# A sketched attention feeding four attention experts on one core: the written-out order of jobs redone at both ends, v spread by ScalarE, more idle matmuls at the start, and the last group finished expert by expert

## The chip, the cores and the metric

The kernel runs on one core of one Trainium2 chip. The metric is the time of one execution on the device in microseconds (us). PE is the matrix engine, DVE the vector engine, ACT the scalar engine, POOL is GpSimd, and SP issues DMAs. SBUF is the on-chip memory that all of them read; PSUM is where PE writes.

## The reference, cut to what matters

```
# block 1, for each batch b (4) and head h (4), S = 1088 rows, D = 32, r = 8
phi(x) = outer(S1 x, S2 x)              # 64 features per row
kv = phi(k)^T v ;  z = sum of phi(k) over the rows
attn = (phi(q) kv) / (phi(q) . z + 1e-6)
x = attn of the 4 heads side by side    # (4, 1088, 128)
# block 2, 4 experts, each row keeps its best 2 of logits = x @ w_gate
a_e = softmax(causal(x wq[e] (x wk[e])^T / 8))
out = sum over the two kept experts of share * (a_e x wv[e] wo[e])
```

The inputs are 32-bit floats; S1 and S2 arrive as 64-bit patterns that the kernel decodes itself.

## The kernel before, in words

**Jobs and their order.** The kernel is a list of 1270 jobs. `job(...)` (line 78) records a job's name, the engine or the engines that may do it, a planned cost, what it reads, what it makes and which buffers it holds. `Plan.run` (line 84) walks the text `ORDER` (line 21): each word is a job's number, with the letter a or b for the first or second of two engines ("-" as engine means that the job is left out). The order of the words is the order in which each engine's instructions stand, and an engine runs its instructions strictly in that order. Waits between engines are put in by the tile framework. The cost and landing figures given to `job` are only what the order was planned with: `run` doesn't use them. All DMAs are issued by SP, except three early ones by ACT.

**Front, batch 0.** `decode` (line 293) turns the bits of S1 and S2 into floats on DVE; `spread1` to `spread3` copy them to the other partitions. `dummy0` to `dummy39` (line 244) are idle matmuls, two 128x512 matmuls each on a tile of zeros; most are left out. k, q and v are loaded (lines 457 to 472); `turn k`, `turn q` transpose on DVE (line 494 and 488), `sketch q0` and `sketch k0` multiply with S on PE (line 518), `back` transposes out of PSUM on DVE (line 522), `features` forms the outer product on DVE or POOL (line 527), one job per head. `sums 0.m` adds up kv and z on PE (line 558): it needs `spread v0` and `spread v1` (line 447), which copy the loaded v into rows of 33 with a one at the end. `turn qf`/`keep qf` (lines 592, 594) turn the features of q, `numer` (line 615), `divide`, `turn x` and `keep x` give x. `turn w`, `keep w`, `products` and `keep M` (lines 378 to 409) fold wq with wk and wv with wo into Mq and Mo.

**Choice of experts.** `logits` (line 807) on PE, then `choose a`, `choose b`, `maximum` and `turn choice` on DVE (lines 827 to 888) and `shares` on POOL. Masks for group 0 of batch 0 are widened on PE by `onehot` (POOL, line 369) and `widen` (line 906); the other masks go through a DRAM tensor `md` and come back by DMA.

**Batches 1 to 3** are prepared beside the scores of the batch before: `sketch`, `features` and `sums` of k, `expand`, `repeat sums`, `fifth` and `keep rep`, `sketch q`, `weigh q`, `invert q`, `scale q`, `features q`, `turn f`, and `numer` (line 757), the PE job that gives x of the next batch.

**Scores and values.** The 17 strips of 64 rows stand in groups 0 (strips 0 to 5), 1 (6 to 11) and 2 (12 to 16). `query`, `base` and `pick` (lines 953 to 985) form the queries of the two chosen experts of each row; for each strip `score` (line 998, PE), `take` (1010, DVE: mask and running minimum), `exp` (ACT), `guard`, `invert` (DVE), `weigh` (1041, POOL) and `turn A` (1046, DVE). `sum b.n.j` (line 1074) multiplies the weights of a group with x on PE. `values` (line 1056) then makes the four experts' parts out of the two PSUM tiles: `keep V` copies, `patch V` overwrites where a row's second expert sits in the other tile, `spread V` multiplies by the masks on POOL, two experts at a time. `outputs` (line 1115) multiplies with Mo: for group 0 `out 3.0.x` does 128 rows with all four experts each (line 1144), then one `keep out` and one `store out`. Batch 3 runs its groups in the order 1, 2, 0, so that `out 3.0` is the end of the kernel.

Of the kernel before, what the change touches and what calls it, by code (L numbers as in the profile page):

```python
# [14 lines left out]
ALU = mybir.AluOpType  # L15
# [6 lines left out]
56 45 47 0 1 8a 77 60 46 3 2 76 25a 19a 17a 48 79 49 51 78 57 90 89 74 87 75 88 50 13b 98 100 99 102a 103a 91 92 83 93  # L22
97a 84 81 104b 22a 101b 113 96a 117 118a 82 111 112a 115 109 110a 94a 95a 38b 80 392 86 85 106 116a 393 114a 105 108a
107a 391 394 402 395 401 405 406 119 404 408a 54 120 124 125 129 407 130 121 66 122a 52 64 58 53 65 146 131 410a 126
411a 67b 132a 400 127a 147 152 55 68 397 396 69 123 71 150 70 148 153 155 44b 398 180 72 27b 16b 684 149 151 167 168
169 170 63 156 157a 158 685 159a 59 409b 179 184a 183a 154 162 163 181 399 185 73 182 413 412 186 414a 61 403 174 687
686 695 694 416 194 62a 415 417 195 196 420b 418b 215 216 419b 217 218a 421 222 423 9b 24b 31b 26b 422 164 219 171 128
165 137 187 188 133 172 246 173 430 431 197a 198 223 424 425 189 190a 191 245 250a 12b 166a 199 688 249a 201 202 200
318 5b 432 160 203 208 175 251 7a 426 427a 433a 224 247 192 428b 248 225a 161a 209 429 434a 210 252 319 322a 323a 193
435 698 268 226 227 700 699 204a 205 206 139 220 135 176 267 269 270 228 436 438a 207 141 703a 271b 704b 437b 324 221  # L30
211a 212 260 261 262 263a 213 275 321 276 277 278 279b 177 178b 214 253 254 456 458 272 457 273 14b 142 693 320 325
255 292 291 293 274 701a 42b 264 691 280 702a 134 136 229 230 231 459 460 692 256b 234a 284 294 283 233a 462 281 257
232a 258 265 690 689 706 705 285 286 235b 342 707a 708 237 236 239 709 710 696 713a 238 711a 712a 259 282 697 461 266
295a 296 343 326 344 297 287a 327 328 288 289 298 714 715 717 463 350 290 329 330b 716 723 724 725 345 346a 10b 143
21b 472 138 331 473 477b 718 347 351 352 35b 353 354a 144 727a 332 348 719 140 29b 439 476b 464 299 300 301 302 303
304 308a 441 306a 307a 726a 333 349 467 478 335 310 474 440 334 305b 309 475 336 479 359 337 338a 358 360 339 361 362
355 468 508 509 442 720a 984 311 312 540 721a 363 340 501 364a 443 502 480 979 341 481 482 541 314 465 487 365 488 356
357 483a 315 313 366 367 538 494 977 978 495 980 316a 981 728 539 542a 368 369 370 987 496 503 504a 145 371 372 373
374 317 469 375 470 543a 544 545 471a 505 506 985 988 484 485 486 497b 444 498 722 499 510 511b 489 490a 491 512 513
376 379b 447 500 380a 515 383 516 553 377a 381 445 554 492 493 378a 382 448 584 585 586 517 518a 729 555 449 446 453  # L40
982 983 730a 514 519 731b 451 991 520 521 993 749 556b 992 994b 587 588a 569 546 996b 750 384 385 997a 507 557 558 547
751 548 386 568 989 522 589 523 524 549a 550 551 559 570 571 526a 752 753 590 242 591 525a 754 611 529 995a 530 241
528b 527a 531 612 616a 561 760 732 452 387 615a 755 455 466 733 572a 756 560 573 574 389 614 562 563 986 613 240 576
577 617 618 620 575 43b 552 532 644 28b 18b 619 578 579 621 243a 580b 581 643 765 652 564a 565 766 769a 582 651 768
757 645 583 636 566 567 390 653 770a 771 635 654 655 627 622 244 623a 761 762 628 637 656 657b 629 630 638 767 772 624
658 659 646 625 592 660 639a 640 631b 641 593 594 450 595 596 597 794 598a 999 647a 632 642 601b 602 648 600a 599a 795
633 634 649 998 736 1000a 603 605 535 626 454 773 774 787 650 534 763 788 533 780 781 808 809 810 811a 764a 536b 812
661 662 789 775 663 813 796 797b 798 790b 604 782 664 665 666 667 1002 814 668 669 990 1005a 734 776b 777 672a 671a
778 1006b 670b 1001 735 739 1003 832 1004a 791 388 799 783b 800 673a 674 675 831 835a 801 784 1007 802 803 1008 792
676 1009 793 836a 834 677 1010 1016 833 904 738 678 742 30b 758 804b 1011 837 1017 785 805 806 759 1012 1018 838 1013a  # L50
905 908a 862 1014a 1020a 909a 807 679 910 878 786 779 737 537 877 879 747 839 840 841 907 906 880 911 861 863 1019a
1021 881b 842a 846 847 682 740 815 816 817 746 864 865a 820a 853 866 867 821a 824 854 1015 868 882 936 819a 823 39b
34b 40b 41b 855 848 849b 937 818a 850 851 856 822 938 1022 1024b 869 1023b 607 843 883 884 939 870 748 871 872 1042
857b 1044 928 680 741 681 844 845 1043 858 606 873a 874 929 608 1045 825 1047 852 930 940a 1046 1048 875 859 860 921
944 945 946 920 743 941 609a 922 610 744 913 931 932a 1049 912 914 947 933 934 942 915 948 876 949 950b 1126 916a 917
951 1125 1053 918 1054 1124 1128b 935 1025 1127 923 952 885 886 943 887 888 889 890 1129a 1051 891a 1130 1131 892b
924a 925 894b 895 828 896 926 898 893a 33b 927 32b 826 953 827 1139 829a 830 4 1147 1140 919 897 1055 1146 1132 1133
1148 1154 1155 1156 1198 1199 1149 1150a 1197 1201a 1134 1052 1027 1141 1142b 1143 1200 954 955 956 957 958 959 1202a
745 1029 1028 1026 1035 683 1037 960 1056 1057b 1135b 1157 1158b 1159 961 962 1203 1204 1213 1136 1137 1170 963a 1144
1145 1160 966a 1161 1171 1214 964a 968 1151 1152 1138 965a 967 1237 1205 1206 1172 1173 1174a 1238 1229 1215 970 969  # L60
1031 1207 1208 1209a 1239 1216 1059 1153 1039 1230 1162 1163 1217a 1240 1058 1231 1164 1061 1210 1211 1165 1241 1060
1063b 1050 1218 1062b 1166b 971 1064 1167 1175 1232 1242 899 1212 972 1168 1065 1176 1177 6b 1233a 1234 1169 1221
1243b 1040 1244 1222 1223 901 1235 1224 1066 900 1038 1067 1068 1245 1246 1219 1033 1069b 902a 1032 1030 1220 1101
1102 973 1178 1179 1034 1087 1225b 1226 1227 1236 1073 1074 1180 1075 1228 1088 1076a 1036 1181 1080 1081 1077 1094
1095 1096 1182 1103 1104b 1183 1184b 1097b 1098 1186b 1089 1090b 1091 1247 1248 1249 976 1187a 1105 1106 1250 1251
1252 1041 1188 1253 1254 1255 1185b 1189 1092 11b 1190 23b 903 1107 36b 1191 1194 1078 1070 1082 1083a 1193 1099 1093
975 1084 1071 1257b 1100 974 1192 1258a 1256a 1079 1085 1260 1261 1263 1259b 1086 1262 1072 1108 1195a 1196 1109 1110
1113a 1114b 1111a 1112b 1116 1117 1115 1264 1265 1267 1268 1266 1118 1120 1119 1121 1122a 15b 1269 1123 37b 20b
# [46 lines left out]
def kernel(  # L115
# [127 lines left out]
    job("table", "ACT", 1.5, lambda e: nc.scalar.activation(out=warm, in_=warm, func=ACTF.Exp), ["room"], rank=-150)  # L243
# [75 lines left out]
    def spread(e, h):  # L319
        copy(e, SK[32 * h : 32 * h + 32], SK[0:32])  # L320
# [5 lines left out]
    for h in range(1, 4):  # L326
        job(f"spread{h}", ("DVE", "POOL", "ACT")[h % 3], (0.12, 0.2, 0.22)[h % 3], lambda e, h=h: spread(e, h), ["ST"], "SKW", rank=-189)
# [87 lines left out]
    def prepare(b, rank):  # L415
# [31 lines left out]
        def spread_v(x):  # L447
            if x == 0:
                nc.gpsimd.tensor_copy(plan[vp][:, 0:N8, :, 0:D].rearrange("p j h d -> p h j d"),
                                      plan[room_v[0]][:, 0 : H * N8 * D].rearrange("p (h j d) -> p h j d", h=H, d=D))  # L450
            else:
                nc.gpsimd.tensor_copy(plan[vp][0:64, N8, :, 0:D],
                                      plan[room_v[1]][0:64, 0 : H * D].rearrange("p (h d) -> p h d", h=H))
# [3 lines left out]
        for x in range(2 if early else 4):  # L457
            job(f"load k{b}.{x}", "SP", 0.45 if early else 0.7, lambda e, x=x: load_k(nc.sync, x), lead,
                ("kin", b, x if early else 0), [kin], landing=1.6 if early else 0.95, rank=rank(-0.1))
# [774 lines left out]
```

## Time and profile before

| what | value |
|---|---|
| median of 3 runs | 279.85 us (279.17, 279.85, 280.01) |
| the profiled execution | 280.91 us, of which span of the instructions 279.2 us |
| PE, DVE, POOL, ACT busy over the span | 94%, 78%, 55%, 36% |
| mean granted PE clock | 0.994 |
| moved by DMA | 27.36 MB |

The profiled execution is 1.06 us over the median; 1.71 us of it lie outside the span. A row of the timeline gives the start and the length in us, the engine (PEld is PE's loading of weights, SPq the DMA issues of SP), the line, the operation, out<-in, the form and the count, and in brackets the engine's idle time just before with who ended it. A 32-bit matmul stands as two records. A row of the table by stretches gives, after the stretch and its length, the busy time of PE, PEld, DVE, ACT and POOL with counts, then the granted clock, the DMA engines' share and GB/s.

### The profile page before, as it was taken

Reading aid. Unit: us, or ns where it says so; the run is one execution under the profiler, and the core shown is the slowest. Engines: PE = TensorE matmul, PEld = TensorE weight load, DVE = VectorE, ACT = ScalarE, POOL = GpSimd, SP = SyncE. Lnnn points to the kernel's source line nnn. Section 1 sums busy time; section 2 is a strip of 40 time slices with the busy share of each in tenths; the row PEclk is TensorE's granted clock in tenths of the full one; section 3 lists DMA queues with packets and bytes.
Section 4 is the critical chain, followed back from the end, with each engine's and each line's share of the span. In section 5 each row is a group of like instructions: output and inputs, shape, how many; then the busy total and the mean of one; then the engine's idle time right before and its main releaser. Section 6 shows DMA issues by size and latency. Waiting matters only on the chain.

```text
span 279.2 us, 9471 instructions
## 1 busy us (share of the span) xinstructions
PE 263.8 (94%) x3953; PEld 194.8 (70%) x3953; DVE 218.8 (78%) x541; ACT 100.2 (36%) x272; POOL 153.3 (55%) x246
## 2 busy tenths in 40 slices
PE   5789899899999999989999999999999999999993
PEld 1478575448486796676589976756696975789973
DVE  4895998999989987998969437999898468986340
ACT  2030346254333444433462331463423335233110
POOL 6323636677789834546565458655447432544570
PEclk9979999999999999999999999999999999999999
DMA  8855749921617879243900166701403756820012
GB/s 179 139 141 102 112 124 258 153 34 24 143 32 120 166 184 180 57 102 65 198 6 4 30 150 141 162 2 38 108 2 76 130 116 133 165 56 5 2 31 52
DMA packets 85547, 27.36 MB, mean 98 GB/s; under 512 B 54080, under 2 KB 84864, under 8 KB 85504
## 3 DMA queue, kind: packets, MB, share of 16 engines
q1 hardware_dynamic: 83280, 26.47, 46.4%
q8 instruction: 31, 0.51, 0.8%
q10 hardware_dynamic: 2224, 0.28, 0.6%
q14 instruction: 12, 0.10, 0.1%
HBM read 22.22 MB, written 4.52 MB: 96 GB/s over the span
## 4 chain that ended last, share of the span: by engine, by line
PE 70%; DVE 20%; issue 5%; POOL 2%; ACT 1%; DMA 1%; DVEq 0%; POOLq 0%
PE pair L1074 24%; PE pair L998 19%; PE pair L960 9%; PE pair L1144 6%; PE pair L518 3%; PE pair L558 3%; DVE AT L1046 2%; DVE w L522 2%; DVE w L1010 2%; DVE fp L527 2%; PE pair L1124 2%; PE pair L615 1%; PE pair L592 1%; DVE in L494 1%; DVE xT L191 1%
## 5 line engine op out<-in xcount | busy, mean ns | idle before, releaser
L1041 POOL TENSOR_SCALAR w<-w,rs,sh 128x384 f32<-128x384 f32 (+15 forms) x68 | 55.6, 824 | 54.8 <-DVE rs L1037 52.0
L998 PE MATMUL pair<-xT,qs 128*128 128x384 f32 (+11 forms) x216 | 76.8, 482 | 1.7 <-DVE agg L191 1.3
L1026 ACT ACTIVATE w<-w,mx 128x640 f32<-128x640 f32 (+15 forms) x68 | 52.4, 770 | 72.3 <-DVE mx L1010 56.6
L998 PEld LDWEIGHTS pair<-xT,qs 128*128 128x128 f32 x216 | 37.7, 190 | 26.9 <-issue 10.0
L1046 DVE STREAM_TRANSPOSE AT<-w 128x576 f32<-128x576 f32 (+13 forms) x68 | 50.6, 758 | 5.4 <-POOL w L1041 5.2
L1010 DVE CUSTOM_DVE_ANT_0 w<-pair,mask 128x768 f32<-128x768 f32 (+13 forms) x68 | 48.3, 721 | 5.4 <-PE pair L998 4.7
L1074 PEld LDWEIGHTS pair<-AT,xra 32*128 32x128 f32 x1136 | 41.6, 185 | 6.0 <-DVE mx L1010 2.6
L1074 PE MATMUL pair<-AT,xra 32*128 32x192 f32 (+5 forms) x1136 | 44.5, 303 | 0.0
L1101 POOL TENSOR_TENSOR agg<-agg,mb 128x768 f32<-128x768 f32 (+1 forms) x24 | 37.3, 1565 | 12.7 <-ACT agg L191 6.6
L960 PE MATMUL pair<-xT,Mq 128*128 128x384 f32 (+1 forms) x96 | 34.9, 478 | 0.1
L527 POOL TENSOR_TENSOR fp<-w 128x576 f32<-128x576 f32 x21 | 25.4, 1224 | 14.2 <-DVE w L522 12.5
L191 ACT COPY agg<-pair 128x384 f32<-128x384 f32 (+1 forms) x33 | 14.0, 462 | 44.2 <-PE pair L1074 37.7
L1074 PE MATMUL pair<-AT,xrb 32*128 32x160 f32 (+5 forms) x752 | 26.9, 287 | 0.3 <-issue 0.3
L1074 PEld LDWEIGHTS pair<-AT,xrb 32*128 32x128 f32 x752 | 26.1, 186 | 1.0 <-issue 1.0
L1144 PEld LDWEIGHTS pair<-Mo,agg 128*128 128x128 f32 x192 | 23.4, 192 | 4.1 <-POOL agg L1101 1.7
L1144 PE MATMUL pair<-Mo,agg 128*128 128x128 f32 x192 | 24.9, 279 | 1.0 <-POOL agg L1101 0.9
L960 PEld LDWEIGHTS pair<-xT,Mq 128*128 128x128 f32 x96 | 17.2, 190 | 11.2 <-issue 3.2
L973 DVE COPY_PREDICATED qs<-mb,pair 128x768 f32<-128x768 uint16 (+1 forms) x24 | 23.0, 960 | 2.4 <-DMA mb<-md 1.8
L191 DVE COPY agg<-pair 128x384 f32<-128x384 f32 (+1 forms) x15 | 7.9, 532 | 13.1 <-PE pair L1074 11.7
L518 PE MATMUL pair<-in,SK 32*32 32x288 f32 x416 | 13.4, 494 | 3.0 <-DVE in L494 3.0
L522 DVE STREAM_TRANSPOSE w<-pair 128x576 f32<-128x576 f32 x16 | 11.6, 756 | 5.6 <-PE pair L518 5.6
L1097 DVE COPY_PREDICATED agg<-mb,pair 128x384 f32<-128x384 uint16 (+1 forms) x24 | 12.6, 550 | 3.3 <-ACT agg L191 2.9
(160 smaller groups left out, 295.4 us busy)
## 6 DMA issues: line engine op xcount, KB each, us to landing
mb<-md SPq DMA_DIRECT2D x7, 576.0 KB, 5.2
xra<-xd SPq DMA_DIRECT2D x16, 192.0 KB, 4.3
xrb<-xd SPq DMA_DIRECT2D x16, 192.0 KB, 3.6
xrc<-xd SPq DMA_DIRECT2D x16, 160.0 KB, 4.9
mb<-md SPq DMA_DIRECT2D x4, 480.0 KB, 5.4
in<-in_k_dram SPq DMA_DIRECT2D x12, 136.0 KB, 4.1
in<-in_q_dram SPq DMA_DIRECT2D x3, 544.0 KB, 5.5
xd<-w SPq DMA_DIRECT2D x12, 136.0 KB, 3.5
```

Source lines behind the costliest of these rows:

```text
L191: (nc.scalar.copy if eng == "ACT" else VEC[eng].tensor_copy)(o, i)
L527: VEC[e].tensor_tensor(out=f, in0=a[:, :, None, R : 2 * R].to_broadcast([128, NJ, R, R]), in1=a[:, :, 0:R, None].to_broadcast([128, NJ, R, ...
L960: nc.tensor.matmul(plan[ps[x]][:, y, 0:w], Mq[:, ((1, 2), (0, 3))[x][y]], plan[xT][:, 64 * t0 : 64 * t1], start=True, stop=True)
L973: nc.vector.copy_predicated(chosen(), rows(c), rows(plan[ps[x]]))
L998: nc.tensor.matmul(plan[p][:, y, 0 : c1 - c0], plan[qs][:, 128 * t : 128 * t + 128], plan[xT][:, c0:c1], start=True, stop=True)
L1010: nc.vector.tensor_tensor_reduce(out=o, in0=src, in1=msk, scale=-1.0, scalar=mx[:, b, i, x - 1 : x] if x else 3e38, op0=ALU.add, op1=ALU.m ...
L1026: nc.scalar.activation(out=a, in_=a, func=ACTF.Exp, bias=mx[:, b, i, last : last + 1], scale=-1.0, accum_out=zs[:, b, i : i + 1])
L1041: nc.gpsimd.tensor_scalar(out=a, in0=a, scalar1=rs[:, b, i : i + 1], scalar2=plan[("sh", b)][:, i : i + 1], op0=ALU.mult, op1=ALU.mult)
L1046: nc.vector.transpose(dst[:, 0 : keys // 32, t], plan[A][:, 0:keys].rearrange("p (j s) -> p j s", s=32))
L1074: nc.tensor.matmul(plan[Vk[g // 2]][:, g % 2, lo : 32 * nt], plan[(f"xr{j // 12}", b)][rows, j % 12], a[rows, j, lo:], start=(j == 0), sto ...
L1101: nc.gpsimd.tensor_tensor(out=a, in0=a, in1=plan[mb][:, 2 * x : 2 * x + 2, 0:w], op=ALU.mult)
L1144: nc.tensor.matmul(plan[p][0:m, 0, 128 * x : 128 * x + 128], plan[agg][:, e, 128 * x : 128 * x + m], Mo[:, e], start=(e == 0), stop=(e == ...
```

## The change

`v spread by ScalarE`: the two `spread v` jobs may run on ACT or POOL. In the new order the large one (128x1024) is still POOL's, the small one (64x128) is ACT's. `table` (an exponential of one element on ACT that loads the function table) is placed early, and `spread2` waits for it. `values` and `outputs` get a branch for group 0 of batch 3 (`last_group`).

```diff
-    job("table", "ACT", 1.5, lambda e: nc.scalar.activation(out=warm, in_=warm, func=ACTF.Exp), ["room"], rank=-150)
+    job("table", "ACT", 1.5, lambda e: nc.scalar.activation(out=warm, in_=warm, func=ACTF.Exp), ["room"], "table", rank=-198)
...
-        def spread_v(x):
+        def spread_v(e, x):
...
-                job(f"spread v{x}", "POOL", 1.2 if x == 0 else 0.3, lambda e, x=x: spread_v(x), [("vl", b)], ("vp", b),
+                job(f"spread v{x}", ("ACT", "POOL"), (0.95, 1.2) if x == 0 else (0.3, 0.3), lambda e, x=x: spread_v(e, x), [("vl", b)], ("vp", b),
...
+        if last_group(b, n):
+            def mix(x):
+                nc.vector.tensor_tensor(out=by_half(plan[agg][:, x]), in0=sums_of(x), in1=by_half(plan[mb][:, x]), op=ALU.mult)
+
+            def scale_one(e, x):
+                a = plan[agg][:, 2 + x, 0:w]
+                VEC[e].tensor_tensor(out=a, in0=a, in1=plan[mb][:, 2 + x, 0:w], op=ALU.mult)
...
+    def last_group(b, n):
+        return b == B - 1 and n == 0
...
+            def project_expert(e, first_, last_):
+                for x in range(3):
+                    nc.tensor.matmul(piece(x), plan[agg][:, e, 128 * x : 128 * x + 128], Mo[:, e], start=first_, stop=last_)
...
+            order = (0, 2, 1, 3)
+            for y, e in enumerate(order):
+                job(f"out {b}.{n}.{e}", "PE", 12 * 0.056, lambda _, e=e, y=y: project_expert(e, y == 0, y == 3),
+                    [("agg", b, n, e), ("M", 1)] + ([("po", b, n, y - 1)] if y else []), ("po", b, n, y), [agg, *ps, ob], mode="F",
...
+            for x in range(3):
+                job(f"keep out {b}.{n}.{x}", ("ACT", "DVE"), (a_us(128), d_us(128)), lambda e, x=x: keep_piece(e, x),
...
+                job(f"store out {b}.{n}.{x}", ("SP", "ACT"), (0.45, 0.45), lambda e, x=x: store_piece(e, x), [("ob", b, n, x)], None, [ob],
```

So in the last group `mix` multiplies straight out of PSUM on DVE for experts 0 and 1, `scale` multiplies experts 2 and 3 after their patch, `out 3.0.e` adds one expert at a time to all three blocks of 128 rows, in the order 0, 2, 1, 3, and the three blocks are copied and stored one by one. The planned costs and landings of some early loads change too; they don't enter the program.

**The order.** From `numer 1` (word 259 before, 260 after) to the sums of the last batch the words are the same, but for a few that swap places. Before that point and after it the order is new. Jobs that change engine:

| job | before | after |
|---|---|---|
| idle matmul jobs before `sketch q0` | 4 | 9 |
| `dummy2` before `query 0.1.1x` | on PE | left out |
| `dummy39` before `turn qf 0.3` | left out | on PE |
| `features q0.2`, `features k0.0` | DVE | POOL |
| `features q0.3`, `features q0.0` | POOL | DVE |
| `keep qf 0.1`, `keep qf 0.3`, `keep sums 0.1`, `base 0.0.1` | ACT | DVE |
| `keep w`, `keep rep 1.0`, `keep rep 1.1`, `keep fifth 1` | DVE | ACT |
| `features k1.1`, `features q1.1` | DVE | POOL |
| `keep V 3.1.3`, `keep V 3.2.1`, `keep V 3.2.3` | DVE | ACT |
| `keep V 3.2.0` | ACT | DVE |

Moves within an engine that the text below uses: on PE `turn w0`, `turn w1`, `turn w2` go from behind `numer 0` to before it, and `sums 1` from behind `query 0.0` to behind `logits 0.0`; on DVE `turn k1.0` stands behind `keep qf 0.1`; on POOL `onehot` goes ahead of `features k1`; on SP `load k0.0` goes behind two loads of v, the loads of w0 to w2 go ahead of those of k1, and the five loads of v1 stand together, behind `load q1` and ahead of the stores of x.

More of the change, by code (lines that the diff above doesn't have):

```diff
@@ L326 @@
     for h in range(1, 4):
-        job(f"spread{h}", ("DVE", "POOL", "ACT")[h % 3], (0.12, 0.2, 0.22)[h % 3], lambda e, h=h: spread(e, h), ["ST"], "SKW", rank=-189)
+        job(f"spread{h}", ("DVE", "POOL", "ACT")[h % 3], (0.12, 0.2, 0.22)[h % 3], lambda e, h=h: spread(e, h), ["ST"] + (["table"] if h == 2 else []), "SKW", rank=-189)
     for x in range(5):
@@ L458, in prepare @@
             job(f"load k{b}.{x}", "SP", 0.45 if early else 0.7, lambda e, x=x: load_k(nc.sync, x), lead,
[L459 removed]
+                ("kin", b, x if early else 0), [kin], landing=0.8 if early else 0.95, rank=rank(-0.1))
         def load_rows():
@@ L465, in prepare @@
             for x in range(4):
-                job(f"load q{b}.{x}", "ACT" if x % 2 else "SP", 0.8, lambda e, x=x: by_head(nc.scalar if e == "ACT" else nc.sync, plan[qin], q, x),
-                    lead, ("qin", b), [qin], landing=0.95, rank=rank(-0.09))
+                job(f"load q{b}.{x}", "ACT" if x % 2 else "SP", 0.42, lambda e, x=x: by_head(nc.scalar if e == "ACT" else nc.sync, plan[qin], q, x),
+                    lead, ("qin", b), [qin], landing=0.85, rank=rank(-0.09))
         else:
@@ L1103, in values @@
         r = rank + 0.1
+        if last_group(b, n):
[4 more added lines that the diff above has]
+                VEC[e].tensor_tensor(out=a, in0=a, in1=plan[mb][:, 2 + x, 0:w], op=ALU.mult)
+            for x in range(2):
+                job(f"keep V {b}.{n}.{2 + x}", ("ACT", "DVE"), (a_us(w), d_us(w)), lambda e, x=x: keep(e, 2 + x),
+                    [("V", b, n)], ("aggk", b, n, 2 + x), [Vk[x], agg], rank=r)
+                job(f"mix V {b}.{n}.{x}", "DVE", d_us(w), lambda _, x=x: mix(x), [("V", b, n), *masks_of(b, n, 0)], ("agg", b, n, x),
+                    [Vk[x], agg, mb], rank=r + 0.01 * x)
+                job(f"patch V {b}.{n}.{x}", "DVE", d_us(w), lambda _, x=x: patch(x),
+                    [("V", b, n), ("aggk", b, n, 2 + x), *masks_of(b, n, 2)], ("aggp", b, n, x), [Vk[1 - x], agg, mb], rank=r + 0.01)
+                job(f"scale V {b}.{n}.{x}", ("POOL", "DVE"), (p_us(w), d_us(w)), lambda e, x=x: scale_one(e, x),
+                    [("aggp", b, n, x), *masks_of(b, n, 1)], ("agg", b, n, 2 + x), [agg, mb], rank=r + 0.02)
+            return
         for x in (2, 3, 0, 1):
@@ L1138, in outputs, with piece, keep_piece, store_piece @@
                     landing=0.35, rank=rank + 0.01)
+            return
+        if last_group(b, n):
+            ps = [("ps", "po", b, n, x) for x in range(2)]
+            def piece(x):
+                return plan[ps[x // 2]][:, x % 2, 0:128]
+            def project_expert(e, first_, last_):
+                for x in range(3):
+                    nc.tensor.matmul(piece(x), plan[agg][:, e, 128 * x : 128 * x + 128], Mo[:, e], start=first_, stop=last_)
+            def keep_piece(e, x):
+                copy(e, plan[ob][:, 128 * x : 128 * x + 128], piece(x))
+            def store_piece(e, x):
+                (nc.scalar if e == "ACT" else nc.sync).dma_start(out=out[b, 64 * t0 + 128 * x : 64 * t0 + 128 * x + 128],
+                                                                in_=plan[ob][:, 128 * x : 128 * x + 128])
+            order = (0, 2, 1, 3)
+            for y, e in enumerate(order):
+                job(f"out {b}.{n}.{e}", "PE", 12 * 0.056, lambda _, e=e, y=y: project_expert(e, y == 0, y == 3),
+                    [("agg", b, n, e), ("M", 1)] + ([("po", b, n, y - 1)] if y else []), ("po", b, n, y), [agg, *ps, ob], mode="F",
+                    rank=rank + 0.001 * y)
+            for x in range(3):
+                job(f"keep out {b}.{n}.{x}", ("ACT", "DVE"), (a_us(128), d_us(128)), lambda e, x=x: keep_piece(e, x),
+                    [("po", b, n, 3)], ("ob", b, n, x), [ps[x // 2], ob], rank=rank + 0.01 + 0.001 * x)
+                job(f"store out {b}.{n}.{x}", ("SP", "ACT"), (0.45, 0.45), lambda e, x=x: store_piece(e, x), [("ob", b, n, x)], None, [ob],
+                    landing=0.37, rank=rank + 0.01 + 0.001 * x)
             return
```

101 lines of the change are left out of this document (51 added, 50 removed).

## Prediction

> **What bounds the kernel now.** I read the table by stretches first, cut where the change cuts the order: the first k, q and x of batch 0 (to 23.16 us), the choice of experts and the first scores (to 54.41, where `back k2` has freed PSUM for `numer 1`), the long part whose order stays, and the end from the last sum on.
>
> ```profile
> 3.79:23.16 19.37, 14.84 (x288) 9.54 (x286) 15.17 (x37) 3.18 (x8) 6.55 (x18) 0.91 0.69 151
> 23.16:54.41 31.25, 28.44 (x365) 19.30 (x365) 28.85 (x85) 12.16 (x38) 17.01 (x34) 1.00 0.82 162
> 54.41:268.78 214.37, 212.38 (x3267) 160.86 (x3265) 171.78 (x414) 82.19 (x222) 123.77 (x180) 1.00 0.43 87
> ```
>
> In the long part PE is busy for 212.38 of 214.37 us: it is bound by PE and keeps its order, so I cost it at nothing and let it shift as a block. From 23.16 to 54.41 DVE (28.85 of 31.25) and PE (28.44) are both nearly full, while ACT (12.16) and POOL (17.01) have room. Second, the stretch's ends and what PE waits for in it:
>
> ```profile
> 23.16 0.78 DVE L522 STREAM_TRANSPOSE w<-pair 128x576 f32<-128x576 f32 x1 [2.86 <-PE pair L518]
> ```
> ```profile
> 52.98 1.43 DVE L522 STREAM_TRANSPOSE w<-pair 128x576 f32<-128x576 f32 x2
> 53.80 2.18 PE L757 MATMUL pair<-fp,kvr 32*32 32x288 f32 x64 [0.90 <-DVE w L522]
> ```
> ```profile
> PE pair L906 <- DVE ch L811: 1.4, 1, 1.4
> ```
>
> DVE has stood idle for 2.86 us before 23.16, waiting for the sketch of k1; from there on it hardly stops, and `numer 1` waits for it at the end. So this stage is DVE's, with PE close behind.
>
> **The change, part by part.**
>
> *The stage 23.16 to 54.41.* What DVE hands away, and one stall:
>
> ```profile
> 28.62 0.95 DVE L191 COPY AT<-pair 128x768 f32<-128x768 f32 x1
> 30.22 1.46 POOL L370 CAST AT<-ident 64x1536 bf16<-64x1536 f32 x1
> 30.23 1.48 DVE L833 TENSOR_TENSOR ch<-ch 128x12 f32<-128x12 f32 x1
> 34.06 0.19 DVE L833 TENSOR_TENSOR ch<-ch 128x22 f32<-128x22 f32 x1
> 35.56 0.71 DVE L527 TENSOR_TENSOR fp<-w 128x576 f32<-128x576 f32 x1
> 36.61 2.29 PE L558 MATMUL pair<-vp,fp 128*64 128x33 f32 x72
> 40.68 0.29 DVE L191 COPY kvr<-pair 128x128 f32<-128x128 f32 x1
> ```
> ```profile
> 47.26 2.83 POOL L527 TENSOR_TENSOR fp<-w 128x576 f32<-128x576 f32 x2
> 47.54 1.50 DVE L527 TENSOR_TENSOR fp<-w 128x576 f32<-128x576 f32 x1
> 47.69 0.59 PE L247 MATMUL pair<-idle 128*128 128x512 bf16 x2 [0.42 <-DVE qs L973]
> ```
> ```profile
> 254.04 0.56 DVE L191 COPY agg<-pair 128x384 f32<-128x384 f32 x1 [1.40 <-PE pair L1074]
> ```
>
> `keep w` 0.95, `features k1.1` 0.71, `features q1.1` 1.50, two `keep rep` 2 x 0.29 = 0.58 leave DVE: 3.74. A compare of 12 elements takes 1.48 there, exactly as long as POOL's `onehot` beside it, and 0.19 elsewhere: with `onehot` moved ahead, 1.29 go. `base 0.0.1` comes in at 0.56. DVE's ledger: -3.74 - 1.29 + 0.56 = **-4.5**. Cover: POOL takes two features (2 x 1.17 by the row below), ACT `keep w` and the small copies; both are half idle here.
>
> [...]
>
> PE's ledger: its wait before `widen` (1.4, behind the compares) goes, so does `dummy2` with the wait that it stood in (0.59 + 0.42), and `turn w` moves out of the stage:
>
> ```profile
> 27.49 0.82 PE L382 MATMUL pair<-ident,AT 128*128 128x128 f32 x6
> 24.09 1.17 POOL L527 TENSOR_TENSOR fp<-w 128x576 f32<-128x576 f32 x1 [8.08 <-DVE w L522]
> ```
>
> 1.4 + 1.0 + 0.8 = **-3.2**. The smaller of the two ledgers counts, because PE's own work stays: -3.2. `sums 1` (2.29) is only moved, from 36.6 to about 30, into what was PE's wait and the time in front of it.
>
> *The first stage, to 23.16.* Nine idle jobs instead of four, 18 matmuls instead of 8, and `sketch q0` behind them.
>
> ```profile
> 1.31 3.59 PE L247 MATMUL pair<-idle 128*128 128x512 bf16 x8 [1.31 <-DVE idle L240]
> 12.81 0.65 PE L247 MATMUL pair<-idle 128*128 128x512 bf16 x2
> ```
> ```profile
> 7.93 2.61 PE pair L518 x64
> ```
> ```profile
> 50.04 1.60 PE L518 MATMUL pair<-in,SK 32*32 32x288 f32 x64
> ```
> ```profile
> 16.00:19.00 3.00, 2.77 (x13) 2.40 (x12) 2.96 (x6) 0.96 (x2) 0.01 (x1) 0.56 0.90 247
> ```
>
> Idle matmuls take 0.45 each at the start and 0.33 at 12.81; a sketch takes 2.61 at 7.93 and 1.60 at 50.04; the granted clock is 0.56 from 16 to 19. So PE runs slowly at the start although the page has 1.00 there. 18 matmuls at 0.45 end at 1.3 + 8.1 = 9.4 if nothing speeds up, and at about 7.5 to 8.4 if it does on the way, when q is transposed anyway. Gain at the first sketch: 2.61 - 1.60 = 1.0, bounds 1.0 faster to 1.5 slower (9.4 against 7.93). [...]
>
> Against this: on DVE the two `keep qf` come in (512 wide, scaled from the 0.56 for 384: 2 x 0.75 = 1.5), one of them ahead of `turn k1.0`, which the sketch of k1 needs; on PE `turn w` 0.82 and `dummy39` 0.65 stand ahead of the sums; `k0` lands behind two loads of v. DVE's 2.86 us of idle takes in the second `keep qf` and part of the rest. Net bounds: -1.0 and +1.5; I take the sketch of k1 **+0.5** late, near the `keep qf` row. Where `spread v1` goes to ACT (64x128, small) POOL gains little, and the sums wait for features, not for v: nothing.
>
> Front: -3.2 + 0.5 = **-2.7**. [...]
>
> *The end.* Rows of before, with the last sum done at 268.78:
>
> ```profile
> 268.78 2.42 PE L1124 MATMUL pair<-agg,Mo 128*128 128x320 f32 x8
> 268.91 1.02 DVE L191 COPY agg<-pair 128x384 f32<-128x384 f32 x2 [3.30 <-PE pair L1074]
> 269.61 3.30 POOL L1101 TENSOR_TENSOR agg<-agg,mb 128x768 f32<-128x768 f32 x2 [1.88 <-ACT agg L191]
> 270.04 1.06 DVE L1097 COPY_PREDICATED agg<-mb,pair 128x384 f32<-128x384 uint16 x2
> 271.24 0.52 DVE L1127 STREAM_TRANSPOSE ob<-pair 128x320 f32<-128x320 f32 x1
> 272.96 2.50 PE L1144 MATMUL pair<-Mo,agg 128*128 128x128 f32 x20 [0.95 <-POOL agg L1101]
> 275.54 0.48 ACT L191 COPY ob<-pair 128x384 f32<-128x384 f32 x1 [5.76 <-issue]
> 276.04 0.39 SPq L1157 DMA_DIRECT2D out_dram<-ob  x1
> ```
> ```profile
> out_dram<-ob SPq DMA_DIRECT2D x1, 192.0 KB, 2.1
> ```
> ```profile
> 25.22 0.56 DVE L624 TENSOR_TENSOR w<-pair,den 128x384 f32<-128x384 f32 x1
> ```
> ```profile
> 16.26 2.77 DVE L527 TENSOR_TENSOR fp<-w 128x576 f32<-128x576 f32 x4
> ```
>
> POOL's two spreads (3.30) hold 20 of the 24 records of `out 3.0` until 272.96. After: from 268.91 DVE does keep 0.51, mix 0.56 (the row of L624, out of PSUM), patch 0.53, mix 0.56: expert 0 is ready at 271.1. `scale` isn't in the trace: 576 elements take 0.69, so 384 between 0.46 and, by the patch, 0.53; I take 0.5. Expert 2 is ready at 271.6, and after `turn out` 0.52, patch and scale expert 3 at 273.1. PE is free at 271.20; 24 records at 2.50/20 = 0.125 are 3.0, 0.75 an expert; expert 3's turn comes at 273.45. So PE no longer waits and ends at 274.2 instead of 275.46. Three `keep out` on DVE at 0.29 with overlaps end at 275.0; the last store is issued at about 275.1 instead of 276.04, -0.9, and lands a little sooner, being a third of 192 KB: -0.2. End: **-1.1**, bounds -0.6 (DVE late by one 0.5 step) to -1.5.
>
> Ahead of 268.78 POOL now weighs strips 0, 1, 3, 4 before `spread V 3.1`. PE had `sum 3.2` to do until 262.8 and stays covered; if the cover went, each us that the spread is late would cost one.
>
> Sum: 280.91 - 2.7 - 1.1 = 277.1 against the profiled execution; that lies 1.06 over the median, so 279.85 - 3.8 = **276.1**.
>
> **The rivals.**
>
> *POOL becomes the front's bound.* For it: a feature on POOL took 1.42 (2.83 for two) at 47.26 against 1.17 alone, and now all four of q1 are POOL's, ahead of the first `weigh`. Against: POOL is 14 us idle in that stage. [...]
>
> *The clock doesn't open before the first sketch.* 9.4 against 7.93: +1.5, and no 1.0; of these 2.5 the DVE idle of 2.86 takes half. 277.4.
>
> *The order does nothing in front*, each stall moving to the next job: only the end, 278.7.
>
> *Slower: v1 comes too late.* `sums 1` now stands on PE before the logits of groups 1 and 2, at about 30 us.
>
> ```profile
> 21.73 0.72 SPq L445 DMA_DIRECT2D vp<-in_v_dram  x1
> ...
> 28.19 1.20 SPq L442 DMA_DIRECT2D vp<-in_v_dram  x1
> ```
> ```profile
> vp<-in_v_dram SPq DMA_DIRECT2D x4, 128.0 KB, 3.6
> ```
>
> Before, the last v1 load was issued at 28.19, 3.6 on the median to landing: after 31.8. If the new order had it there, PE would stall 1.8 with everything behind it. It decides from 30 + 3.8 = 33.8: a load issued after 30.2 makes the kernel slower, one us for one; at 35.8 it is 281.9. Against it: the five loads now stand together behind the sums that free the buffer (21.6), about 0.8 us each, so the last is issued near 25.5.
>
> **How the numbers follow.** Forecast 0.62; POOL 0.12; clock 0.09; nothing in front 0.09; v1 late 0.08. The range: 274.5 (DVE's ledger of -4.5 + 0.5 with an end of -1.3) to 278.8 (only the end); v1 late and a little below stay outside. About 0.3% (0.8 us) is what can be told from no change. Faster by more: 0.62 + 0.12 + 0.09 and half of 'nothing in front', 0.875; within: 0.055; slower: 0.07.
>
> **What would show it.** Right: `sketch q0` near 1.6 us; no compare over 0.5 us on DVE; PE's wait at `widen` under 0.5; `numer 1` starts near 51.1 instead of 53.80; from the last sum to the last store issue 6.3 us instead of 7.26, with PE without a wait in between. Wrong: PE waiting for the DMA of v1 or k0; DVE idle behind POOL's features from 38 to 46; a long part that is longer than 214.4 us, so that the shift is given back.

## The result and the profile after

| what | before | after |
|---|---|---|
| median of 21 runs each | 279.85 us (278.97 to 281.25) | 277.85 us (276.38 to 280.42) |
| ratio, 95% interval | | 0.9929 (0.9914 to 0.9943) |
| the profiled execution, its span | 280.91, 279.2 us | 277.85, 276.1 us |
| mean granted PE clock in it | 0.994 | 1.000 |

The change saves 2.0 us; 3.75 were forecast, and the range of 274.5 to 278.8 holds the time. The two profiled executions differ by 3.1 us, which is more than the medians do. That of before lies 1.06 over its median. That of after is one of the 3 in 21 whose mean granted clock is 1.000; the other 18 have 0.987 to 0.993. So the profiles show where time moved; how much it was worth is settled by repeated runs, below. Executions that lie more than 1.5% over the fastest of their kernel are left out of all medians and ratios here.

Up to line 1097 the lines of the changed kernel are numbered one higher than those of before. First the changed kernel's table by stretches, cut at the start of `numer 0`, of `sketch q1` and of `numer 1`, and then the same three points in the kernel before (columns: length, PE, PEld, DVE, ACT, POOL, clock, DMA share, GB/s):

```profile
23.09:36.27 13.18, 12.99 (x187) 10.68 (x182) 9.80 (x43) 3.88 (x15) 5.66 (x8) 1.00 0.65 120
36.27:52.17 15.90, 14.02 (x174) 7.84 (x173) 14.62 (x37) 7.13 (x21) 11.36 (x27) 1.00 0.87 170
```
```profile
23.09:41.14 18.05, 16.68 (x208) 12.98 (x204) 16.74 (x52) 5.93 (x17) 8.64 (x20) 1.00 0.62 122
41.14:53.80 12.66, 11.22 (x160) 6.26 (x159) 11.50 (x31) 6.23 (x23) 8.35 (x15) 1.00 1.08 217
```

Both kernels reach `numer 0` at 23.09 in these two executions. From there the changed one is at `sketch q1` 4.87 us sooner, and at `numer 1` only 1.63: 3.24 are given back in between. The first half is now PE's (12.99 busy of 13.18, DVE 9.80). In the second DVE is the fuller (14.62 of 15.90, PE 14.02). PE's timeline of the changed kernel:

```profile
1.24 5.35 PE L248 MATMUL pair<-idle 128*128 128x512 bf16 x18 [1.24 <-DVE warm L238]
7.96 1.62 PE L519 MATMUL pair<-in,SK 32*32 32x288 f32 x64 [1.37 <-DVE in L495]
...
15.57 2.23 PE L593 MATMUL pair<-ident,fp 128*128 128x128 f32 x14 [2.64 <-DVE fp L528]
...
46.28 0.81 PE L999 MATMUL pair<-xT,qs 128*128 128x320 f32 x2 [0.59 <-ACT mb L192]
...
50.46 1.24 PE L999 MATMUL pair<-xT,qs 128*128 128x288 f32 x4 [0.55 <-DVE qs L974]
...
52.17 1.77 PE L758 MATMUL pair<-fp,kvr 32*32 32x288 f32 x64
```

The idle matmuls end at 6.6 and the first sketch takes 1.62 us instead of 2.61. Then PE pauses for 2.64 us before `turn qf`. The wait of 1.4 at `widen` is down to 0.4; scores now wait for picks and masks (0.55, 0.59). On DVE the compare that took 1.48 beside `onehot` takes 0.14:

```profile
31.56 0.14 DVE L833 TENSOR_TENSOR ch<-ch 128x12 f32<-128x12 f32 x1
```

The end, from PE's, DVE's and SP's timelines:

```profile
267.39 2.42 PE L1146 MATMUL pair<-agg,Mo 128*128 128x320 f32 x8
269.67 2.92 PE L1172 MATMUL pair<-Mo,agg 128*128 128x128 f32 x24
```
```profile
268.05 0.55 DVE L1107 TENSOR_TENSOR agg<-pair,mb 128x384 f32<-128x384 f32 x1
269.45 0.54 DVE L1111 TENSOR_TENSOR agg<-agg,mb 128x384 f32<-128x384 f32 x1
```
```profile
273.14 0.83 SPq L1178 DMA_DIRECT2D out_dram<-ob  x2
```

`mix` (0.55) and `scale` (0.54) keep ahead of PE, which has no wait after the last sum. The second of the last two issues on SP starts about 273.58: 6.19 us behind the last sum at 267.39, where it was 7.26.

### The profile page after: what moved, and what is told of

Its sections match the earlier page's. It is cut to its first block, busy times and chain, and to the rows that moved or that the text cites. A ratio compares the mean times of both kernels' runs of the same rounds, so it can differ in the third digit from the quotient of the medians.

```text
span 276.1 us, 9491 instructions
## 1 busy us (share of the span) xinstructions
PE 261.8 (95%) x3961; PEld 193.7 (70%) x3961; DVE 217.5 (79%) x543; ACT 99.4 (36%) x271; POOL 153.8 (56%) x247
## 4 chain that ended last, share of the span: by engine, by line
PE 63%; DVE 22%; DMA 4%; issue 4%; ACT 3%; POOL 2%; SPq 1%; DVEq 0%; ACTq 0%; POOLq 0%
PE pair L1075 24%; PE pair L999 18%; PE pair L961 6%; PE pair L1196 6%; DVE AT L1047 3%; DVE w L1011 2%; DVE w L523 2%; DVE fp L528 2%; DVE qs L974 2%; DMA in<-in_k_dram 2%; DMA xra<-xd 2%; PE pair L1146 2%; PE pair L559 2%; PE pair L519 1%; PE pair L1172 1%
## 5 line engine op out<-in xcount | busy, mean ns | idle before, releaser
L1042 POOL TENSOR_SCALAR w<-w,rs,sh 128x896 f32<-128x896 f32 (+15 forms) x68 | 55.9, 829 | 55.0 <-DVE rs L1038 53.0
L1027 ACT ACTIVATE w<-w,mx 128x640 f32<-128x640 f32 (+15 forms) x68 | 52.4, 771 | 69.2 <-DVE mx L1011 54.1
L1047 DVE STREAM_TRANSPOSE AT<-w 128x576 f32<-128x576 f32 (+14 forms) x68 | 50.7, 758 | 5.9 <-POOL w L1042 5.5
L1102 POOL TENSOR_TENSOR agg<-agg,mb 128x768 f32<-128x768 f32 (+1 forms) x22 | 34.1, 1561 | 11.7 <-ACT agg L192 6.6
L528 POOL TENSOR_TENSOR fp<-w 128x576 f32<-128x576 f32 x23 | 27.1, 1194 | 8.2 <-DVE w L523 8.0
L1196 PEld LDWEIGHTS pair<-Mo,agg 128*128 128x128 f32 x168 | 20.6, 192 | 2.4 <-issue 1.3
L1196 PE MATMUL pair<-Mo,agg 128*128 128x128 f32 x168 | 21.6, 278 | 0.0
L192 DVE COPY agg<-pair 128x384 f32<-128x384 f32 (+1 forms) x12 | 6.4, 533 | 12.7 <-PE pair L1075 7.6
L1035 POOL TENSOR_SCALAR rs<-zs 128x1 f32<-128x1 f32 x31 | 6.6, 213 | 17.0 <-ACT w L1027 13.9
L1038 DVE RECIPROCAL rs<-rs 128x1 f32<-128x1 f32 x68 | 8.8, 143 | 7.8 <-POOL rs L1035 5.9
```

The costliest lines, as they stand in the source:

```text
L192: (nc.scalar.copy if eng == "ACT" else VEC[eng].tensor_copy)(o, i)
L528: VEC[e].tensor_tensor(out=f, in0=a[:, :, None, R : 2 * R].to_broadcast([128, NJ, R, R]), in1=a[:, :, 0:R, None].to_broadcast([128, NJ, R, ...
L1027: nc.scalar.activation(out=a, in_=a, func=ACTF.Exp, bias=mx[:, b, i, last : last + 1], scale=-1.0, accum_out=zs[:, b, i : i + 1])
L1042: nc.gpsimd.tensor_scalar(out=a, in0=a, scalar1=rs[:, b, i : i + 1], scalar2=plan[("sh", b)][:, i : i + 1], op0=ALU.mult, op1=ALU.mult)
L1047: nc.vector.transpose(dst[:, 0 : keys // 32, t], plan[A][:, 0:keys].rearrange("p (j s) -> p j s", s=32))
L1102: nc.gpsimd.tensor_tensor(out=a, in0=a, in1=plan[mb][:, 2 * x : 2 * x + 2, 0:w], op=ALU.mult)
```

## Experiments

Times are medians; the ratio, with its 95% interval, is to runs of the kernel before on the same chip. The medians of before in these sets lie between 279.6 and 280.1, so medians of different sets compare to no better than about 0.4 us. Each edit is given in words of the order (job number and engine letter); jobs are named beside it.

**The two halves apart.** The changed front with the old end (before's words from the last sums on, too):

```diff
-        return b == B - 1 and n == 0
+        return False
```

> The new order up to numer 1 and spread v1 on ACT, with the last group and all that follows as before. Theory A (both halves gain, by what the two profiles show: the first sum 1.54 us earlier, of which 0.15 is given back by the last one): numer 1 starts near 52.2, the last sum of the last group is done near 267.4, the time is 1.0 to 1.5 us under before, 278.4 to 278.9. Rival B (the profile of before was a slow one by 1.06 us and the front's real gain is only what is left of 1.4): 0 to 0.6 us under before, 279.3 to 279.9. Rival C (the front gains the 2.7 that I forecast and the end is what fell short): 277.1.

279.73 us, 0.9989 (0.9966 to 1.0012), the time of rival B. And the old front with the new end (before's words up to `numer 1`, after's from there):

> The order of before up to numer 1 with spread v on POOL, then the last group expert by expert. Theory A: the stretch from the last sum to the last store issue is 6.2 us instead of 7.26 and the end lands 0.6 sooner, so 1.1 to 1.7 us under before, 278.2 to 278.8. Rival B: the end is the whole gain, 277.9 to 278.2. Rival C: the end gives nothing that the median shows, 279.5 to 279.9.

278.70 us (278.78 over all twelve executions), 0.9954 (0.9931 to 0.9977), the time of theory A. So the end alone saves about 1.2 us, as forecast. The front saves about 0.2 where it stands alone and 0.9 beside the new end, not 2.7; the first interval reaches from 1.0 us faster to 0.3 slower, so the two don't contradict each other.

**The idle matmuls.** The changed kernel with four of the nine jobs:

```diff
-13a 22a 24a 27a 31a
+13b 22b 24b 27b 31b
```

> The changed kernel with only four idle matmul jobs ahead of the first sketch, as before the change; the other five are left out. If the idle matmuls open the clock: the first sketch takes 2.6 us again instead of 1.62, back q starts 1.0 later, and as DVE is busy from 6.5 to 23.1 with 1.6 us of idle, 0.4 to 1.0 us reach the end: 278.3 to 278.9. Rival (the order hides it, as DVE waits for k0 from the DMA at 9.6 anyway): the sketch is slow and the time is within 0.3 us of the changed kernel, 277.6 to 278.1.

278.61 us, 0.9948 (0.9927 to 0.9968): 0.76 slower than the changed kernel by the medians and 0.5 by the ratios, whose intervals overlap. The first sketch takes 2.61 again, and `numer 0` starts at 25.07. Then the counterpart, the old front with nine jobs (five more "a" behind the fourth) and the new end:

> The order of before up to numer 1 with nine idle matmul jobs instead of four ahead of the first sketch, and the new end. If the idle matmuls alone are the front's gain, and the new order gives nothing: 277.7 to 278.1, as fast as the changed kernel. If the order is what gains: the first sketch takes 1.6 us instead of 2.6, the time is 278.3 to 278.9, about that of the new end alone (278.78).

277.79 us, 0.9921 (0.9905 to 0.9937): as fast as the changed kernel, 0.9 under the old front with four. Each pair alone is near the edge of its intervals, but both point the same way: the five idle jobs carry the front's gain, and the new order beside them adds nothing that shows. This kernel has both `spread v` on POOL, so the move of the small one to ACT, which wasn't run by itself, adds nothing that shows either. PE in the old order with nine:

```profile
13.32 0.33 PE L593 MATMUL pair<-ident,fp 128*128 128x128 f32 x1 [1.66 <-POOL fp L528]
...
21.85 2.89 PE L616 MATMUL pair<-kvz,fp 128*128 128x66 f32 x24
...
52.58 2.18 PE L758 MATMUL pair<-fp,kvr 32*32 32x288 f32 x64 [0.91 <-DVE w L523]
```

Here `numer 0` starts at 21.85. From there to `numer 1` it takes 30.73, as before (30.71). The new order starts `numer 0` 1.2 to 1.5 later than this and regains 1.6.

**One stall of the ledger put back.** `dummy2` on PE before `query 0.1.10` in the changed kernel:

```diff
-7b
...
-247a
+7a 247a
```

> The changed kernel with the idle job dummy2 on PE again before query 0.1.10. By my ledger of PE (0.59 of work and the wait in front of it): numer 1 starts 0.6 to 1.0 later, 278.4 to 278.9. If DVE is the bound from 38 us on, as the trace of the changed kernel has it (PE waits for picks there, 0.55 us right behind that place): the job falls into the wait, within 0.3 us of the changed kernel, 277.6 to 278.1.

278.15 us, 0.9944 (0.9922 to 0.9966). The median is 0.3 over the changed kernel and does not tell the two apart; PE's rows do:

```profile
23.38 1.33 PE L616 MATMUL pair<-kvz,fp 128*128 128x66 f32 x10
...
47.23 0.59 PE L248 MATMUL pair<-idle 128*128 128x512 bf16 x2
...
52.48 1.78 PE L758 MATMUL pair<-fp,kvr 32*32 32x288 f32 x64
```

With 0.59 us more to do PE needs 29.10 us from `numer 0` to `numer 1`, against 29.08 without. The job falls into a wait: in the changed order it costs nothing. In the old order it wasn't left out by itself.

**Two features back on DVE.**

```diff
-409a 428a
+409b 428b
```

> The changed kernel with features k1.1 and features q1.1 on DVE again, at the same places in the order. If DVE is the bound of the stage from the first scores to numer 1: features q1.1 (0.7 to 1.5 us) shows in full, numer 1 starts 0.7 to 1.5 later and the time is 278.5 to 279.3; features k1.1 falls into DVE's 2.1 us of idle before turn logits and costs nothing. If POOL's chain (weigh q, scale q, four features) is the bound: the time falls by up to 1.2, 276.7 to 277.6. If PE is the bound: within 0.3 us, 277.6 to 278.1.

278.78 us, 0.9954 (0.9932 to 0.9976). DVE's row of `features q1.1`, and PE's of `numer 1`:

```profile
44.81 0.96 DVE L528 TENSOR_TENSOR fp<-w 128x576 f32<-128x576 f32 x1
```
```profile
53.43 1.77 PE L758 MATMUL pair<-fp,kvr 32*32 32x288 f32 x64
```

`numer 0` started at 23.68, so the stage took 29.75, 0.67 more. DVE is the bound there, POOL is not. By the medians the two features cost 0.9, by the ratios 0.7, with intervals that overlap.

**The pause before `turn qf`.** Three idle jobs in it:

```diff
-113a
+5a 19a 7a 113a
```

> The changed kernel with three more idle matmul jobs (six matmuls, about 1.8 us) on PE in its pause of 2.6 us before turn qf 0.2. Theory (the pause decides whether the granted clock halves for one window of 3.4 us between 14 and 21 us, which costs about 1.1 us by the profile with features k1.1 and q1.1 on DVE, where sums 0 starts at 19.92 instead of 18.82): the clock stays at 1.0 in every profile and run, the time is 276.7 to 277.3. Rival (the dip is hidden by the features on DVE and POOL, or the idle jobs hold up turn qf): 277.6 to 278.4.

279.39 us, 0.9967 (0.9949 to 0.9986), slower than either expectation. One row of PE's waits from 6 to 24 us (us in total, times, the longest):

```profile
PE pair L248 <- DVE w L523: 2.9, 1, 2.9
```

The second idle job was given a PSUM buffer that DVE's `back` still read, and held PE back: `turn qf` started at 17.33 instead of 15.57. The pause wasn't filled, and the mean granted clock of the profile is 0.994 where the changed kernel's is 1.000. What a filled pause is worth wasn't measured.

**Where the first stage loses, where the second gains.** Three kernels. The hybrid has before's order with nine idle jobs up to `numer 0`, then the changed one, the new end, and `turn w` behind `numer 0`:

> The order of before up to numer 0 with nine idle jobs, then the changed order, and the new end; turn w0 to w2 and keep w stand behind numer 0 (their loads ahead of those of k1). Theory (the new order loses 1.5 us ahead of numer 0 and wins 1.6 from there to numer 1, by the traces of the old front with nine idle jobs, 21.85 and 52.58, and of the changed kernel with dummy2, 23.38 and 52.48): numer 0 starts near 21.9, numer 1 near 51.7 (21.9 + 29.1 and 0.8 for turn w), the time is 276.8 to 277.3. Rival (what is early at numer 0 is given back by waits behind it): numer 1 at 52.2 or later, 277.6 to 278.2.

277.50 us, 0.9918 (0.9896 to 0.9940), between the two expectations. The trace is the rival's: `numer 0` starts at 22.84, not 21.9, and `numer 1` at 52.51. The reverse has the changed order up to `numer 0`, then before's:

> The changed order up to numer 0, then that of before up to numer 1 (with dummy2), and the new end. Theory: numer 0 near 23.3, from there 30.7 less the 0.8 of turn w, which stands ahead: numer 1 at 53.0 to 53.4, the time is 278.4 to 279.0. Rival (the gain of the changed stage comes only from what stood ahead, onehot and turn w): numer 1 near 52.4, 277.7 to 278.1.

278.49 us, 0.9945 (0.9926 to 0.9965): the theory's time. But its profile has `numer 1` at 52.21, sooner than the rival's 52.4, where the changed kernel has 52.17:

```profile
22.90:52.21 29.31, 27.15 (x360) 18.54 (x356) 25.76 (x82) 12.12 (x38) 13.95 (x27) 1.00 0.83 156
```

With `onehot`, `turn w` and `keep w` taken out ahead, even the old order needs only 29.31 instead of 30.71. So 1.4 of the 1.63 come with what stands ahead of `numer 0`, by the profile. The two features and the two `keep rep` are on DVE again here, 2.79 us of my ledger for DVE, and the stage is only 0.23 longer than in the changed kernel. The median is 0.6 over the changed kernel with overlapping intervals, so that this stays half settled. The third is the changed kernel with before's engines for the features of q0 and k0:

```diff
-102a 104a
+102a 103a 104b
...
-101a
+101b
...
-103b
...
-94b
+94a
```

> The changed kernel with the features of q0 and k0 on the engines of before: q0.1, q0.2 and k0.0 on DVE, q0.3 and q0.0 on POOL. Theory (turn qf waits 1.9 us longer in the changed order because DVE makes three features of q one after the other, 3.89 us, and POOL one): turn qf starts at 13.3 to 13.8 instead of 15.2 to 15.6, numer 0 0.6 to 1.2 us earlier, the time is 276.6 to 277.3. Rival (keep qf on DVE and turn w1 with dummy39 on PE are what holds the sums): numer 0 within 0.3 us of 23.1 to 23.4, 277.5 to 278.1.

277.94 us, 0.9931 (0.9910 to 0.9951). My theory fell: `turn qf` starts at 14.70, but `numer 0` at 23.45, no sooner. DVE shows why, and so does the hybrid's; first the kernel with the split back, then DVE and POOL of the hybrid:

```profile
15.00 4.98 DVE L528 TENSOR_TENSOR fp<-w 128x576 f32<-128x576 f32 x4
```
```profile
15.35 4.55 DVE L528 TENSOR_TENSOR fp<-w 128x576 f32<-128x576 f32 x4
```
```profile
15.55 1.46 POOL L371 CAST AT<-ident 64x1536 bf16<-64x1536 f32 x1
16.96 3.09 POOL L347 COPY rep<-ident 32x128 f32<-32x128 f32 x4
```

The four features of k0 take 4.98 and 4.55 us, beside POOL's copies `rep16`, `onehot` and `rep4` (the `rep` jobs are small copies); before the change four took 2.77 in the row at 16.26, with POOL idle behind 16.0. So `onehot` had been moved out of the way of a compare (1.48 us down to 0.14) and here stands in the way of the features.

**The copies in POOL's idle time.** The hybrid, with these three ahead of `features q0.3`, where POOL was idle for 4.1 us:

```diff
-104b
+63 58 59 104b
...
-59 63 58
```

> The order of before to numer 0 with nine idle jobs, then the changed one (as the hybrid before it), with onehot, rep4 and rep16 on POOL ahead of features q0.3, in POOL's 4.1 us of idle time, instead of behind spread v. Theory (POOL's copies lock DVE's features of k0 there: 4.55 us for four instead of 2.76): the four take 2.8 us again, numer 0 starts 0.9 to 1.0 earlier at 21.9, numer 1 at 51.5, the time is 276.5 to 277.1. Rival (the lock moves to DVE's transposes of q and k at 6.6 to 9.6, or the gain is given back behind numer 0): numer 1 at 52.2 or later, 277.4 to 278.0.

**276.41 us, 0.9886 (0.9862 to 0.9910)**: 3.3 under the kernel before, and 1.2 (by the ratios) to 1.4 under the changed kernel, whose interval (0.9914 to 0.9943) it just doesn't touch. Against the hybrid, from which it differs in the place of the copies alone, it is 1.1 by the medians, with intervals that overlap. DVE, POOL and PE of it:

```profile
15.08 2.77 DVE L528 TENSOR_TENSOR fp<-w 128x576 f32<-128x576 f32 x4
```
```profile
6.41 1.46 POOL L371 CAST AT<-ident 64x1536 bf16<-64x1536 f32 x1
7.82 1.27 POOL L347 COPY rep<-ident 32x128 f32<-32x128 f32 x4
```
```profile
20.99 3.67 PE L616 MATMUL pair<-kvz,fp 128*128 128x66 f32 x31
...
50.59 1.77 PE L758 MATMUL pair<-fp,kvr 32*32 32x288 f32 x64
```

The features take 2.77 again and POOL's four copies 1.27 instead of 3.09: both sides had paid. `numer 0` starts at 20.99 instead of 22.84 in the hybrid, `numer 1` at 50.59 instead of 52.51. That is more than the 1.0 expected, by what DVE's features gave (1.78), and the time is 0.1 under the range expected. Of the 1.92 at `numer 1`, 1.41 are left at the end of the last sum (265.58 against 266.99).

**The last store.** The same kernel, `store out 3.0.1` on ACT:

```diff
-1126a
+1126b
```

> The kernel with onehot early, and the store of the second 128 rows of the last group issued by ACT instead of SP, where two stores stand one behind the other. By the rows of the changed kernel (two issues on SP take 0.83 us, the second starts 0.44 after the first): the last issue starts 0.1 to 0.2 us sooner, the time is 0.1 to 0.2 us under the kernel with onehot early, which only the traces can tell. Rival (the landing, not the issue, is the end): nothing, or up to 0.2 slower.

276.62 us, 0.9886 (0.9861 to 0.9911): nothing, as the rival had it. From PE's last matmul to the end of the span it takes 3.59 us, in the kernel without this edit 3.54.

## Why the forecast was right in direction and half off in size

- **The end (-1.1)** was right: the end alone gives -1.2, with 6.19 us for the 6.3 expected from the last sum to the last issue, and no wait of PE.
- **The first stage (+0.5)** came out near as a sum: `sketch k1` starts at 21.56 where it was 21.55, and at 21.85 in the kernel with `dummy2`, so 0.0 to 0.3 late. The gain booked in it was right: the nine idle jobs give 1.0 at the first sketch (1.62 us) and 1.2 at `sketch k1` in the old order (20.32). That more idle matmuls quicken the first sketch was an estimate of mine, which no row of before shows; the runs show 2.61 us behind eight of them and 1.62 behind eighteen. What I booked as +1.5 for `keep qf`, `turn w` and late loads is a loss of nearly that size (1.2 to 1.5: 23.09 and 23.38 against 21.85 at `numer 0`), but I named its causes at best in part: in the hybrid, which has no `keep qf` on DVE, the three copies alone cost 1.85 (22.84 against 20.99). That the two nearly cancel, as booked, is in part luck.
- **The step that failed** is "The smaller of the two ledgers counts, because PE's own work stays: -3.2". It measured -1.6. DVE's ledger was roughly true as a count: DVE has 24.42 us of work left of 28.24 (-3.8 for -4.5). But the stage has two halves with different bounds, and a stall that goes in one is worth only what the other engine has in hand. PE's waits from `numer 0` to `numer 1`, in the old order (the kernel with nine idle jobs) and in the changed one, show it:

```profile
PE pair L907 <- DVE ch L812: 1.4, 1, 1.4
PE pair L758 <- DVE w L523: 0.9, 1, 0.9
PE pair L248 <- DVE qs L974: 0.4, 1, 0.4
```
```profile
PE pair L999 <- DVE qs L974: 0.7, 2, 0.6
PE pair L999 <- ACT mb L192: 0.6, 1, 0.6
PE pair L907 <- DVE w L523: 0.4, 1, 0.4
PE pair L631 <- DVE w L625: 0.2, 1, 0.2
PE pair L961 <- DVE w L523: 0.2, 1, 0.2
```

  I took 1.4 and 0.4 as won. 2.7 us of waits became 2.1. Of the terms, `dummy2` (1.0) was worth nothing in the changed order, and `turn w` 0.5 to 0.6 instead of 0.8: the stage takes 29.67 and 29.60 with it, 29.10 without.
- **The signs I named**: the first sketch is at 1.62, the compare at 0.14, the wait at `widen` at 0.4; only `numer 1` missed, 52.17 for 51.1. The idle matmuls ended at 6.6, sooner than my 7.5 to 8.4: behind 3.8 us they follow each other at 0.22, where the row that I had read gave 0.33. The long part takes 215.29 from `numer 1` to the end of the last sum (215.05 before), so 0.2 was given back there.
- **The rivals.** POOL isn't the bound: its two features back on DVE cost 0.7 to 0.9. The clock does open before the first sketch: behind 3.8 us the idle matmuls follow each other at 0.22 instead of 0.43, and the sketch takes 1.62. v1 isn't late: `sums 1` starts at 30.46 with no wait. The measured 277.85 lies nearer to "the order does nothing in front" (278.7) than to the forecast, and about the order as such that rival is right. The range holds the time because it reached up to that rival; the forecast itself is off by 1.75.
- **DVE beside POOL.** The sum counts what DVE loses beside POOL at one place only, the compare beside `onehot` (1.29). The runs show it at another too, where products on DVE stand beside plain copies on POOL (4.55 us for the four features of k0 instead of 2.77), and there it was worth 1.9 us at `numer 1` and 1.1 of the median.
- **What stays open.** Between two profiles with a lowered clock (mean 0.991 and 0.994), the kernel with `dummy2` and the one before, `numer 1` comes 1.3 sooner (52.48 for 53.80), and 1.2 go at the end: 2.5, where the medians have 2.0. The profile of before lies 1.06 over its median, and in which part isn't known. Why the reverse kernel's median is higher than its profile says wasn't settled either.

## What to carry to other kernels

When both engines of a stage are nearly full, cut it where the next hand-over between them stands and make a ledger for each piece: a stall that goes on one engine is worth only what the other one has in hand behind it. Before moving a copy on POOL out of one DVE product's way, look at what DVE does at the new place; here POOL's idle time while DVE transposes was free (1.37 us for the two transposes of q beside `onehot` and without it). And test a bundle by its smallest part: here five idle matmul jobs carried all that the new order of the front seemed to bring.

## What the runs showed of the hardware

**When the clock opens.** The trace's record of the granted clock starts at 12.94 us in the kernel before and at 3.89 in the changed one; ahead of it the table prints 1.00 for want of a record. The matmuls show more: in the changed kernel the idle ones that start up to 3.8 us follow each other at 0.43 us, those behind at 0.22. Behind these eighteen the first sketch took 1.62 us. Behind the eight of before, which ended at 4.9, it took 2.61. In the changed kernel with four idle jobs the table has 1.00 from 4.58 to 8.00 and 0.50 from there to 11.41, and the sketch, at 7.95, took 2.61 as well.

**When it closes.** In the kernel before, the granted clock is recorded as 1.00 from 12.94 us, 0.50 from 16.35 and 1.00 again from 19.77: stretches of 3.41 us. With `dummy2` it is 0.50 from 15.20 to 18.61, as long but at another time. I call such stretches windows; in the changed kernel, whose clock is 1.00 from 3.89 to the end of the span, they are counted on from 3.89. Two windows in a row from each of five kernels: first the kernel before, then the changed kernel, the one with `dummy2`, the one with the last store on ACT, and the old front with the new end (length, PE busy first; the clock is the third number from the end):

```profile
12.94:16.35 3.41, 1.91 (x9) 0.73 (x9) 3.38 (x5) 0.26 (x1) 3.07 (x3) 1.00 0.67 135
16.35:19.77 3.42, 3.42 (x28) 3.09 (x28) 3.42 (x6) 1.36 (x4) 0.00 (x0) 0.50 0.72 190
```
```profile
14.13:17.54 3.41, 1.93 (x14) 1.46 (x15) 3.38 (x4) 1.17 (x3) 2.03 (x3) 1.00 0.91 160
17.54:20.95 3.41, 3.41 (x80) 3.04 (x79) 3.41 (x6) 1.26 (x4) 3.41 (x5) 1.00 0.35 131
```
```profile
11.79:15.20 3.41, 0.81 (x19) 0.20 (x2) 3.41 (x4) 0.00 (x0) 2.79 (x2) 1.00 0.68 102
15.20:18.61 3.41, 3.37 (x16) 3.37 (x17) 3.38 (x5) 1.63 (x4) 2.65 (x3) 0.50 0.96 231
```
```profile
9.87:13.28 3.41, 1.59 (x65) 0.62 (x34) 3.38 (x4) 0.00 (x0) 3.19 (x5) 1.00 0.97 150
13.28:16.70 3.42, 2.71 (x18) 1.94 (x18) 3.38 (x6) 0.96 (x2) 1.75 (x2) 1.00 0.98 226
```
```profile
13.13:16.54 3.41, 1.99 (x10) 0.90 (x9) 3.38 (x5) 0.37 (x1) 2.89 (x3) 1.00 0.74 187
16.54:19.95 3.41, 3.41 (x34) 3.08 (x32) 3.41 (x6) 1.58 (x4) 0.00 (x0) 0.50 0.56 129
```

Windows in which PE is busy for 0.81, 1.91 and even 1.99 us of 3.41 are followed by one at 0.50; after windows with 1.93 and 1.59 the clock stays at 1.00. So the busy time of the trace doesn't decide it alone, and what does isn't known from these runs. In the changed order the place of PE's pause of 2.64 us before `turn qf` goes with it in two profiles. With `dummy2` all but 0.04 of the pause (12.60 to 15.24) lies in one window, and the next is at 0.50; in the changed kernel the border at 14.13 splits it into 1.20 and 1.44, and the clock stays. With four idle jobs it doesn't: PE was idle for 1.61 us of the window to 14.82 and for 0.93 behind it, and from 14.82 to 21.65 the clock was 0.50.

**What a lowered window costs.** The three executions of the changed kernel at 1.000 took 276.38, 276.68 and 277.85 us, with a mean 0.9 under the median of all, but they are few and 1.5 us apart. In its order `numer 0` starts at 22.90 to 23.09 in profiles without a lowered window and at 23.38 and 23.68 in two with one. With the copies early (the store on SP) no cost shows: the one execution at 1.000 took 276.02 us, the five at 0.993 and 0.994 from 275.98 to 276.74.

**DVE beside POOL.** POOL's plain copies and DVE's products (the features of k0) both took longer side by side in the hybrid than apart in the kernel with the copies early: 4.55 us instead of 2.77 on DVE, 3.09 instead of 1.27 for the four copies on POOL. DVE's transposes of q took 1.37 beside `onehot` and without it. Products on both engines, the features of q0 in the kernel before:

```profile
11.43 2.83 POOL L527 TENSOR_TENSOR fp<-w 128x576 f32<-128x576 f32 x2 [4.41 <-DVE w L522]
```
```profile
12.04 2.82 DVE L527 TENSOR_TENSOR fp<-w 128x576 f32<-128x576 f32 x2
```

Two on each engine, side by side, take 2.8 us; DVE alone made the four of k0 in 2.77, with POOL idle. Sharing them gained nothing here; whether the kernel is as fast with all four on DVE wasn't run.

**Idle matmuls.** An idle matmul isn't always free: in the experiment on the pause one waited 2.9 us for DVE's reading of the PSUM buffer that it was given, and `turn qf` behind it started at 17.33 instead of 15.57. `dummy2` fell into a wait and cost nothing (29.10 us for the stage, 29.08 without).
